# One tuned kernel, attention into a feed-forward layer: a planner that reckons with the SBUF port, q loads in five slots, weight sums in other slots

## The chip, the cores and the metric

The kernel runs on one core of one Trainium2 chip. The metric is the time of one execution on the device in microseconds (us); of several runs the median counts. TensorE (PE) multiplies, VectorE (DVE) and ScalarE (ACT) work elementwise, GpSimd (POOL) reduces over partitions here, and SyncE (SP) issues all DMAs. SBUF is the memory that these engines share, PSUM the memory that TensorE writes to; tiles lie in a fixed number of slots of a tag, and a tile waits until a slot of its tag is free.

## The reference

```
q, k, v: [8, 8, 576, 64]      w_phi: [64, 128]      w_in: [512, 2048]   w_out: [2048, 512]  (float64)

phi(x):  proj = x @ w_phi;  proj -= max|proj| over the 128 features
         return concat(exp(proj), exp(-proj))                     # 256 features
q_p, k_p = phi(q), phi(k)
kv  = sum over s of k_p[s] (x) v[s];   z = sum over s of k_p[s]
num = q_p @ kv;   den = q_p . z + 1e-6;   attn = num / den         # [8, 8, 576, 64]

x = attn as [4608, 512]
out = gelu(x @ w_in) @ w_out                                       # [4608, 512]
```

## The kernel before, in words

**Attention** goes batch by batch. For K (`k_quad`, from line 392) a quad of four heads has five units: TensorE projects into `pk`, VectorE takes the maximum `mx` (L430) and subtracts it (L334, into `pk` itself in the first two batches and into `ek` in the later ones), ScalarE takes two exponentials (`ek`, L447) and TensorE sums `kv`. For Q (`q_pair`, from line 473) a half of a pair of heads is loaded into `qt` and projected into `pq`; ScalarE copies it to `pc`, GpSimd takes the maximum over partitions (`mb`, L513), VectorE subtracts (`pc`), ScalarE takes two exponentials (`ef`, L519) and TensorE forms `pn`. From the third batch on VectorE first splits q into two parts (`qh`), GpSimd also sums over partitions (`db<-un`, L548), and `pk` and `pq` both use the one PSUM slot `pp`. `quotients` (L568, L569) sends the denominators through DRAM and takes the reciprocal `dc`.

**Feed-forward.** 32 weight tiles arrive as float64 and are turned into two float32r parts by `split_weight` (two steps on ScalarE, five on VectorE: `wt`, `w_i`, `w_o`). A block of 256 tokens loads the attention output (`xr`) and the quotients (`rb`), multiplies and splits them on VectorE (`xr`, `xh`, `xl`), and then does eight steps: 24 matmuls `ph`, two gelu on ScalarE (L635, L636), the difference `gl` on VectorE, and 12 matmuls `po`. Twelve blocks (0 to 11) go this way. The last three wide blocks of 512 tokens save matmuls with sums of weights: `combos` (line 660) builds them on VectorE (`sw`, `sh`), writes them to DRAM (`s_d`), and the wide blocks read them back into a ring (`s<-s_d`) and form `pa` and `pb`.

**What sets the order.** Every operation is first put into a list with an estimated cost and a rank. `Plan.order` plays this list through once at build time: for each engine it takes, among the operations that could start first, the one of lowest rank, and notes a start. `emit` then writes the program of every engine in the order of these starts, and nothing reorders it on the chip. In this play `start_of` (line 136) says when an operation could start, and `taken` lists the spans of the GpSimd operations. A VectorE operation marked `psum` works from PSUM; one that isn't and meets such a span is charged `BLOCKED` = 0.9 us, once for each span. The numbers at the end of the file set ranks, paces and earliest starts: `T15` and `LEAD` how far attention runs ahead of the blocks, `WPACE` the pace in which weights are released, `WR` and `WSPAN` their ranks, `TF` the earliest start of block 0, `EARLY` a shift in rank of the q side of the first batch.

Of the kernel before, what the change touches and what calls it, by code (L numbers as in the profile page):

```python
# [10 lines left out]
F32 = mybir.dt.float32  # L11
F32R = mybir.dt.float32r
# [15 lines left out]
P = 128  # L28
HS = S // 2
# [30 lines left out]
class Plan:  # L60
# [30 lines left out]
    def op(self, eng, cost, fn, r=(), w=(), also=(), rank=0.0, table=None, late=0.0, kb=0, duty=1.0, kind="f", psum=False):  # L91
        o = Op()
        o.eng, o.cost, o.fn, o.rank, o.table, o.late, o.n = eng, cost, fn, rank, table, late, len(self.ops)
        o.users, o.ready, o.nbytes, o.duty, o.kind, o.psum = [], self.since, kb, duty, kind, psum
        deps = set()
        for b in r:
            deps.update(b.writers)
        for b in w:
            deps.update(x for x in b.writers if eng != "sp" or x.eng != "sp")
            deps.update(b.readers)  # L100
        for b in r:
            b.readers.append(o)
        for b in w:
            b.writers.append(o)
        o.bufs = list(dict.fromkeys([*r, *w, *also]))
        for b in o.bufs:
            b.left += 1
        deps.update(self.gate)
        o.deps = deps
        o.wait = len(deps)  # L110
        for d in deps:
            d.users.append(o)
        if eng == "pe" and self.stream in ("k", "q"):
            o.rank += PULL
        self.ops.append(o)
        return o

    def order(self, bias):
# [17 lines left out]
        def start_of(o):  # L136
            t = max(clock[o.eng], o.ready)
            if o.table == "exp" and table[0] == "gelu" and gelus[0] % (2 * STICK):
                t = max(t, left_at[0] + PATIENCE)
            seen = {}  # L140
            for b in o.bufs:
                if not b.held and b.tag is not None:
                    f, i = slot_free_at[b.tag], seen.get(b.tag, 0)
                    if len(b.line) <= i or b.line[i] is not b:
                        return None
                    when = f[(turn[b.tag] + i) % len(f)]
                    if when is None:
                        return None
                    t = max(t, when)
                    seen[b.tag] = i + 1  # L150
            return t


# [2 lines left out]
        taken = []  # L156
# [16 lines left out]
        while len(done) < n:  # L173
            best = None
            for e, lst in cand.items():
# [3 lines left out]
                for o in lst:  # L179
                    t = start_of(o)  # L180
# [26 lines left out]
            _, t, o = best  # L207
            cand[o.eng].remove(o)
            cost = o.cost
# [3 lines left out]
            if o.eng == "pe":  # L213
                if self.SHAPE[last[0]] != self.SHAPE[o.kind]:
                    cost += self.BEHIND[last[0]] + self.BEFORE[o.kind]
                last[0] = o.kind
            if o.eng == "dve" and not o.psum:
                for span in taken[-4:]:
                    if t < span[1] - 0.3 and t + cost > span[0] + 0.3 and not span[2]:
                        span[2] = True  # L220
                        cost += BLOCKED
            if o.eng == "pool":
                taken.append([t, t + cost, False])
            o.start, o.end = t, run(t, cost, o.duty) if o.eng == "pe" else t + cost
            if o.nbytes:
                dge[0] = max(dge[0], t) + 0.55
# [6 lines left out]
            for b in o.bufs:  # L233
                if b.tag is not None and not b.held:
                    f = slot_free_at[b.tag]
# [53 lines left out]
def fused_kernel(ctx: ExitStack, tc: tile.TileContext, qT, kT, va, w_st, w_in, w_out, out):  # L289
    nc = tc.nc  # L290
# [11 lines left out]
    sb = {t: plan.pool(spool, t, n) for t, n in SLOTS.items()}  # L302
    PS = dict(pp=1, kv=1, pn=1, ph=2, po=1)
    ps = {t: plan.pool(ppool, t, n, False) for t, n in PS.items()}
    op = plan.op
# [167 lines left out]
    def q_pair(b, p, kvs, rank, halves=(0, 1)):  # L473
# [4 lines left out]
        for half in halves:  # L478
            nm = f"{b}_{p}_{half}"
            ss = slice(half * HS, half * HS + HS)  # L480
            qt = sb["qt"]([P, HS] if b < EB else [P, 2, HS], F32, f"qt_{nm}")
            if b < EB:
                op("sp", 0.06, lambda qt=qt, ss=ss: nc.sync.dma_start(out=qt(), in_=qT[b, p, :, ss]), w=[qt], kb=147, **k(1))
            else:
                for i in range(2):
                    op("sp", 0.06, lambda qt=qt, ss=ss, i=i: nc.sync.dma_start(
                        out=qt()[64 * i : 64 * i + 64], in_=qT[b, p, :, ss].rearrange("(j d) t -> d j t", j=2)), w=[qt], kb=147, **k(1))
# [4 lines left out]
            pc = sb["pc"]([P, 2, HS], F32, f"pc_{nm}")  # L492
            mb = sb["mb"]([P, 2, HS], F32, f"mb_{nm}")
# [24 lines left out]
            for s in range(2):  # L518
                op("act", act(2 * HS), lambda ef=ef, pc=pc, s=s: nc.scalar.activation(ef()[:, s], pc(), AF.Exp, scale=1.0 - 2.0 * s),  # L519
                   r=[pc], w=[ef], table="exp", **k())  # L520
# [139 lines left out]
    def combos(rank):  # L660
        plan.stream = "c"
        lo, hi = slice(0, 256), slice(256, 512)
        for q in range(4):
            for i in range(2):
                k = dict(rank=rank((2 * q + i) / 8))
                ws = [sb["ob"]([P, 512], F32, f"sw_{q}_{i}_{x}") for x in range(2)]
                hs = [sb[tag]([P, 512], F32R, f"sh_{q}_{i}_{tag}") for tag in ("db", "qt")]
                for x in range(2):
                    c = wi[i + 2 * x, q]
                    tt("dve", dve(512), ws[x], lambda c=c: c()[:, 0].bitcast(F32), lambda c=c: c()[:, 1].bitcast(F32), ALU.add, [c], [ws[x]], also=[*ws, *hs], **k)  # L670
                a, b = ws
                for to, x, y, o in (((b, hi), (b, hi), (a, hi), ALU.add), ((a, hi), (a, lo), (a, hi), ALU.subtract),
                                    ((a, lo), (b, hi), (a, lo), ALU.subtract), ((b, lo), (b, lo), (a, lo), ALU.subtract)):
                    tt("dve", dve(256), lambda to=to: to[0]()[:, to[1]], lambda x=x: x[0]()[:, x[1]], lambda y=y: y[0]()[:, y[1]], o,
                       list({x[0], y[0]}), [to[0]], **k)
                for x in range(2):
                    h, w = hs[x], ws[x]
                    copy("dve", dve(512, fast=True), h, w, [w], [h], **k)
                    tt("dve", dve(512), lambda w=w: w().bitcast(F32R), w, lambda h=h: h().bitcast(F32), ALU.subtract, [w, h], [w], **k)
                    for z, part in enumerate((h, w)):  # L680
                        for y in range(2):
                            op("sp", 0.06, lambda q=q, i=i, x=x, y=y, z=z, part=part: nc.sync.dma_start(
                                out=s_d[q]()[2 * x + y, :, :, i, z, :].rearrange("e p n -> p e n"),
                                in_=part()[:, 256 * y : 256 * y + 256].bitcast(F32).rearrange("p (e n) -> p e n", e=2)), r=[part], w=[s_d[q]], kb=131, **k)
# [3 lines left out]
    def wide_block(j, rank):  # L688
# [55 lines left out]
        for u in range(NU):  # L744
# [3 lines left out]
            sm = {}  # L748
            for s in (2, 3, 1, 4):
                m = sm[s] = sb[RING[s - 1]]([P, 2, 2, P], F32R, f"s{s}_{j}_{u}")  # L750
                op("sp", 0.06, lambda m=m, q=q, e=e, s=s: nc.sync.dma_start(out=m().bitcast(F32), in_=s_d[q]()[SUMS.index(s), e]), r=[s_d[q]], w=[m], kb=262, rank=rk - 20)
            A = ps["ph"]([P, 2, TB], F32, f"pa_{j}_{u}")
            Bk = ps[("kv", "pn")[u % 2]]([P, 2, TB], F32, f"pb_{j}_{u}")
            own = lambda c, f, q=q: (lambda i, w: wi[c + i, q]()[:, w, f % 4 * P : f % 4 * P + P], [wi[c, q], wi[c + 1, q]])
# [105 lines left out]
CR = 100.0  # L860
CSPAN = 100.0
GATE = 60
T15 = 901.4
BIAS = 40
STICK = 2
PATIENCE = 2.5
URGE = -1000.0
EARLY = 37.5
WPACE = 3.996
WSPAN = 24.5  # L870
WARM = 4
EARLY_PK = ("pp", "po")
EARLY_E = ("ek", "xh", "ek", "xl")
BLOCKED = 0.9
HOLD2 = 0.0
EB = 2
KB = 0
EPACE = 20.0
TF = 90.0
ND = 2  # L880
LUMP = 2.5
LINGER = 3.0
PAIR_K = 0.43
PAIR_Q = 0.7
PAIR_N = 1.18
PAIR_V = 0.125
PULL = -2000.0
LEAD = 167.4
HOLD = 44.6
WR = -13.5  # L890
ATR = -21.1
T0 = 57.4
VERBOSE = False


# [36 lines left out]
```

## Time and profile before

| | us |
|---|---|
| median of 3 runs | 1150.15 (1148.31 to 1151.35) |
| the profiled execution | 1147.43 |
| its span, first to last instruction | 1145.7 |
| TensorE busy | 1097.1 |
| VectorE busy | 696.2 |
| ScalarE busy | 662.2 |
| GpSimd busy | 321.5 |

TensorE is busy for 96% of the span. The mean over the span hides stages: up to 112 us there is only attention of the first batches and weight splitting, from there to some 780 us feed-forward blocks and attention are mixed, and then the feed-forward part is alone. A row of a timeline gives start, length, engine, line, operation, tiles and count, and in brackets how long the engine stood idle in front of it and what it waited for. The profile counts most fp32 matmuls twice (two passes of one instruction); the order counts them once.

### The profile page before, as it was taken

The page shows a single profiled execution, that of the slowest core. Times are in us where ns is not written, and L with a number is a line of the kernel's source. Part 1 is how long each engine was busy: PE and PEld are TensorE (multiplying, and loading weights), DVE is VectorE, ACT ScalarE, POOL GpSimd, SP SyncE. Part 2 cuts the span into 40 slices and gives each one's busy share as a digit, 9 for nine tenths or more (in the row PEclk, how much of TensorE's full clock was granted, in tenths as well). Part 3 has the DMA queues.
Part 4 walks back from the last instruction along what each step waited for, and adds up shares of the span by engine and source line. Part 5 has one row for each costly group of instructions (what it writes and reads, how often), then busy time and mean ns, then how long its engine had stood idle before and what let it go on. Part 6 is the DMA issues. An engine that isn't in the chain of part 4 may idle for free.

```text
span 1145.7 us, 22254 instructions
## 1 busy us (share of the span) xinstructions
PE 1097.1 (96%) x8952; PEld 920.4 (80%) x8952; DVE 696.2 (61%) x1153; ACT 662.2 (58%) x1045; POOL 321.5 (28%) x116
## 2 busy tenths in 40 slices
PE   7878987999999999999999999999999999999997
PEld 4545766888887888888888888889889888898986
DVE  6897889665856867656466566554655534534331
ACT  5776857767777787776878778762112222222322
POOL 3323023343644546352445445450000000000000
PEclk9998987999999999999999999999999999999999
DMA  7676631324141332413132231205543624623420
GB/s 248 222 230 215 198 104 33 95 64 129 48 124 43 93 83 86 106 62 102 55 93 80 79 88 49 69 18 125 152 129 115 190 84 115 196 94 114 136 83 37
DMA packets 112439, 125.59 MB, mean 110 GB/s; under 512 B 27648, under 2 KB 87200, under 8 KB 112336
## 3 DMA queue, kind: packets, MB, share of 16 engines
q1 hardware_dynamic: 112336, 124.17, 36.6%
q8 instruction: 70, 1.15, 0.4%
q14 instruction: 33, 0.27, 0.1%
HBM read 96.57 MB, written 27.56 MB: 108 GB/s over the span
## 4 chain that ended last, share of the span: by engine, by line
PE 72%; DVE 9%; DMA 6%; issue 4%; SPq 3%; ACT 3%; POOL 2%; DVEq 0%; ACTq 0%; POOLq 0%
PE po L308 18%; PE ph L308 18%; PE kv L308 6%; PE pb L308 5%; PE po_pp L308 5%; PE pn L308 5%; PE po_po L308 5%; PE pa L308 4%; PE pq L308 3%; PE pk L308 3%; POOL mb L513 1%; SPq L708 1%; DMA qt<-in_qT_dram 1%; DMA rp<-r_d 1%; DVE gl L334 1%
## 5 line engine op out<-in xcount | busy, mean ns | idle before, releaser
L308 PE MATMUL ph<-xh,w_i 128*128 128x256 f32 x1536 | 299.9, 284 | 1.6 <-DVE gl L334 1.2
L308 PEld LDWEIGHTS ph<-xh,w_i 128*128 128x128 f32 x1536 | 248.2, 190 | 9.6 <-issue 2.2
L308 PE MATMUL po<-w_o,gh 128*128 128x512 f32 x768 | 246.4, 402 | 1.9 <-ACT ob L328 1.9
L513 POOL PARTITION_ALL_REDUCE mb<-pc x64 | 147.8, 2311 | 285.6 <-ACT pc L328 247.1
L548 POOL PARTITION_ALL_REDUCE db<-un x48 | 175.3, 3652 | 161.6 <-DVE un L545 123.4
L308 PE MATMUL ph<-xl,w_i 128*128 128x256 f32 x768 | 218.7, 285 | 0.0
L308 PEld LDWEIGHTS po<-w_o,gh 128*128 128x128 f32 x768 | 137.7, 190 | 31.4 <-issue 2.2
L308 PE MATMUL po<-w_o,gl 128*128 128x512 f32 x384 | 152.9, 398 | 0.6 <-DVE gl L334 0.6
L308 PEld LDWEIGHTS ph<-xl,w_i 128*128 128x128 f32 x768 | 146.1, 190 | 3.3
L519 ACT ACTIVATE ef<-pc 128x576 f32<-128x576 f32 x128 | 83.1, 680 | 59.1 <-DVE pc L334 58.8
L334 DVE TENSOR_TENSOR gl<-ph,gh 128x512 fp32r<-128x512 f32 x96 | 65.8, 686 | 84.5 <-ACT ph L636 81.2
L308 PEld LDWEIGHTS kv<-vt,ek 128*64 128x64 f32 (+1 forms) x2560 | 85.6, 140 | 36.7 <-ACT ek L447 14.1
L635 ACT ACTIVATE gh<-ph 128x512 fp32r<-128x512 f32 x96 | 57.5, 599 | 90.5 <-PE ph L308 83.1
L308 PE MATMUL kv<-vt,ek 128*64 128x65 f32 (+1 forms) x2560 | 97.7, 228 | 9.6 <-ACT ek L447 9.3
L308 PE MATMUL pn<-ef,kvn 128*64 128x288 f32 (+1 forms) x512 | 98.1, 425 | 1.2 <-ACT xo L328 1.0
L635 ACT ACT_TABLE_LOAD x76 | 97.5, 1283 | 1.5 <-PE ph L308 0.3
L308 PEld LDWEIGHTS po<-w_o,gl 128*128 128x128 f32 x384 | 73.0, 190 | 18.5 <-DVE gl L334 1.6
L794 ACT ACTIVATE gh<-pa 128x512 fp32r<-128x512 f32 x24 | 14.4, 599 | 123.1 <-PE po_pp L308 86.1
L447 ACT ACTIVATE ek<-ek 128x512 f32<-128x512 f32 (+1 forms) x120 | 70.1, 587 | 24.8 <-DVE ek L334 23.0
L334 DVE TENSOR_TENSOR pc<-pc,mb 128x576 f32<-128x576 f32 x64 | 65.4, 1021 | 29.7 <-POOL mb L513 29.4
L430 DVE TENSOR_REDUCE mx<-pk 128x4 f32<-128x512 f32 (+1 forms) x80 | 50.5, 631 | 50.2 <-PE pk L308 50.0
L308 PEld LDWEIGHTS pn<-ef,kvn 128*64 128x64 f32 (+1 forms) x512 | 39.6, 139 | 32.5 <-issue 7.5
(90 smaller groups left out, 1699.5 us busy)
## 6 DMA issues: line engine op xcount, KB each, us to landing
s<-s_d SPq DMA_DIRECT2D x96, 256.0 KB
qt<-in_qT_dram SPq DMA_DIRECT2D x112, 144.0 KB
vt<-in_va_dram SPq DMA_DIRECT2D x16, 585.0 KB
kt<-in_kT_dram SPq DMA_DIRECT2D x16, 576.0 KB
out_dram<-ob SPq DMA_DIRECT2D x36, 256.0 KB
raw_i<-in_w_in_dram SPq DMA_DIRECT2D x16, 512.0 KB
raw_o<-in_w_out_dram SPq DMA_DIRECT2D x16, 512.0 KB
x_d<-xo SPq DMA_DIRECT2D x48, 144.0 KB
```

Source lines behind the costliest of these rows:

```text
L308: return tc.keep_in_program_order(nc.tensor.matmul(*a, **kw))
L334: op(eng, cost, lambda: e.tensor_tensor(out=dst(), in0=a(), in1=b(), op=o), r=r, w=w, **kw)
L430: op("dve", dve(256 * n, True), lambda xs=xs, mx=mx: nc.vector.tensor_reduce(out=mx()[:, 0].rearrange("p (j i) -> p j i", j=2), in_=xs(), ...
L447: op("act", act(256 * n, b < SB), lambda at=at, es=es, s=s: nc.scalar.activation(es[s](), at(), AF.Exp, scale=1.0 - 2.0 * s), r=[of], w=[e ...
L513: op("pool", 2.2, lambda mb=mb, pc=pc: nc.gpsimd.partition_all_reduce(mb(), pc(), P, bass_isa.ReduceOp.absmax), r=[pc], w=[mb], **k(1))
L519: op("act", act(2 * HS), lambda ef=ef, pc=pc, s=s: nc.scalar.activation(ef()[:, s], pc(), AF.Exp, scale=1.0 - 2.0 * s), r=[pc], w=[ef], ta ...
L548: op("pool", 3.7, lambda db=db, un=un: nc.gpsimd.partition_all_reduce(db(), un(), P, bass_isa.ReduceOp.add), r=[un], w=[db], **k())
L635: op("act", act(2 * TB, True) + 0.016, lambda gh=gh, ph=ph: nc.scalar.activation(gh(), ph(), AF.Gelu), r=[ph], w=[gh], table="gelu", rank= ...
L708: op("sp", 0.06, lambda b=b, i=i, h=h, s=s, n=n, o=o, z=z, to=rp[z]: nc.sync.dma_start(out=to()[64 * i : 64 * i + 64, :, o : o + n], in_=r ...
L794: op("act", act(2 * TB, psum) + 0.016, lambda gh=gh, at=at: nc.scalar.activation(gh(), at(), AF.Gelu), r=[at], w=[gh], table="gelu", rank= ...
```

## The change

The planner no longer charges `BLOCKED`. Instead a VectorE operation that is not marked `psum` cannot start, in the planner's play, inside the span of the GpSimd operation before it; it starts at that span's end. These spans are now 1.4 us for a maximum (`LOCK_MAX`) and 2.4 us for a sum (`LOCK_SUM`), in place of the whole cost of 2.2 or 3.7. The q loads of the first two batches take turns in the tags qt (one slot), gh (two) and gl (two), where they all used qt. The weight sums move from the slots ob, db and qt to ek, mb and pc, and a load of the ring now comes behind the writes of all four parts of the sums, where it came behind the one that it reads. Eleven numbers of the planner change, and with them the order on every engine. (`HOLD` has no effect, since the first two batches start at once.)

```diff
@@ start_of
+            if o.eng == "dve" and not o.psum and taken and taken[-1][0] <= t < taken[-1][1]:
+                t = taken[-1][1]
             return t
@@ order
-            if o.eng == "dve" and not o.psum:
-                for span in taken[-4:]:
-                    if t < span[1] - 0.3 and t + cost > span[0] + 0.3 and not span[2]:
-                        span[2] = True
-                        cost += BLOCKED
             if o.eng == "pool":
-                taken.append([t, t + cost, False])
+                taken.append((t, t + (LOCK_MAX if cost < 3.0 else LOCK_SUM)))
@@ q_pair
-            qt = sb["qt"]([P, HS] if b < EB else [P, 2, HS], F32, f"qt_{nm}")
+            qt = sb[("qt", "gh", "gl")[(2 * p + half) % 3] if b < EB else "qt"]([P, HS] if b < EB else [P, 2, HS], F32, f"qt_{nm}")
@@ combos
-                ws = [sb["ob"]([P, 512], F32, f"sw_{q}_{i}_{x}") for x in range(2)]
-                hs = [sb[tag]([P, 512], F32R, f"sh_{q}_{i}_{tag}") for tag in ("db", "qt")]
+                tags = ("ek", "ek") if i == 0 else ("mb", "pc")
+                ws = [sb[tag]([P, 512], F32, f"sw_{q}_{i}_{x}") for x, tag in enumerate(tags)]
+                hs = [sb[tag]([P, 512], F32R, f"sh_{q}_{i}_{x}") for x, tag in enumerate(tags)]
@@ wide_block
-                op("sp", 0.06, lambda m=m, q=q, e=e, s=s: nc.sync.dma_start(out=m().bitcast(F32), in_=s_d[q]()[SUMS.index(s), e]), r=[s_d[q]], w=[m], kb=262, rank=rk - 20)
+                op("sp", 0.06, lambda m=m, q=q, e=e, s=s: nc.sync.dma_start(out=m().bitcast(F32), in_=s_d[q]()[SUMS.index(s), e]), r=s_d, w=[m], kb=262, rank=rk - 20)
@@ numbers
-T15 = 901.4
+T15 = 1004.363
-LEAD = 167.4
+LEAD = 223.014
-BLOCKED = 0.9
+LOCK_MAX = 1.4
+LOCK_SUM = 2.4
...
```

Three places show how the order moves. The first is SyncE's queue at the start of the program: `kt` and `vt` are K and V of a quad, `qt` a half of a pair of q, `raw` a weight tile. Before:

```order
L321 DMA wst_68<-in_w_st_dram 128x128
L483 DMA qt_0_0_0_70<-in_qT_dram 128x288
L399 DMA kt_0_0_72<-in_kT_dram 128x1152
L401 DMA vt_0_0_74<-in_va_dram 128x1170
L399 DMA kt_0_1_76<-in_kT_dram 128x1152
L401 DMA vt_0_1_78<-in_va_dram 128x1170
L349 DMA raw_i0_0_80<-in_w_in_dram 128x512
L349 DMA raw_i1_0_89<-in_w_in_dram 128x512
L349 DMA raw_i2_0_97<-in_w_in_dram 128x512
L483 DMA qt_0_0_1_106<-in_qT_dram 128x288
```

and now, from the same place:

```order
L318 DMA wst_68<-in_w_st_dram 128x128
L396 DMA kt_0_0_70<-in_kT_dram 128x1152
L398 DMA vt_0_0_72<-in_va_dram 128x1170
L396 DMA kt_0_1_74<-in_kT_dram 128x1152
L398 DMA vt_0_1_76<-in_va_dram 128x1170
L480 DMA qt_0_0_0_78<-in_qT_dram 128x288
L480 DMA qt_0_0_1_80<-in_qT_dram 128x288
L480 DMA qt_0_1_0_82<-in_qT_dram 128x288
L480 DMA qt_0_2_0_85<-in_qT_dram 128x288
L346 DMA raw_i0_0_87<-in_w_in_dram 128x512
```

The first q load moves behind four K and V loads, and four q loads now stand together in front of the weights.

The second place is VectorE in block 0, around the last unit of the first quad of batch 2: `dc_1_0` is the reciprocal that `rb_2` carries to `xr_2`, and `ek_2_0_4` the subtraction that frees the PSUM slot `pp`. Before:

```order
L569 RECIPROCAL dc_1_0_1654<-dc_1_0_1654 128x18
L355 TENSOR_SCALAR wt_o10_1673<-wt_o10_1673 128x512
L334 TENSOR_TENSOR gl_0_3_1713<-ph_0_3_1638,gh_0_3_1683 128x512
...
L334 TENSOR_TENSOR w_o10_1749<-wt_o10_1673,w_o10_1749 128x512
L334 TENSOR_TENSOR xr_2_1554<-xr_2_1554,rb_2_1459 128x1024
L334 TENSOR_TENSOR gl_0_4_1790<-ph_0_4_1715,gh_0_4_1755 128x512
L353 TENSOR_SCALAR wt_o11_1797<-wt_o11_1797 128x512
L355 TENSOR_SCALAR wt_o11_1797<-wt_o11_1797 128x512
L430 TENSOR_REDUCE mx_2_0_4_1811<-pk_2_0_4_1792 128x4
L357 SCALAR_TENSOR_TENSOR wt_o11_1797<-raw_o11_1199,wt_o11_1797 128x512
L334 TENSOR_TENSOR ek_2_0_4_0_1823<-pk_2_0_4_1792,mx_2_0_4_1811 128x512
```

and now:

```order
L427 TENSOR_REDUCE mx_2_0_4_1599<-pk_2_0_4_1550 128x4
L356 SCALAR_TENSOR_TENSOR wt_o8_1521<-raw_o8_1413,wt_o8_1521 128x512
L350 TENSOR_SCALAR wt_o9_1597<-wt_o9_1597 128x512
L331 TENSOR_TENSOR ek_2_0_4_0_1614<-pk_2_0_4_1550,mx_2_0_4_1599 128x512
...
L566 RECIPROCAL dc_1_0_1601<-dc_1_0_1601 128x18
...
L331 TENSOR_TENSOR ek_2_1_1_0_1916<-pk_2_1_1_1860,mx_2_1_1_1892 128x512
L331 TENSOR_TENSOR w_i1_3_1908<-wt_i1_3_1830,w_i1_3_1908 128x512
L352 TENSOR_SCALAR wt_i2_3_1890<-wt_i2_3_1890 128x512
L331 TENSOR_TENSOR xr_2_1686<-xr_2_1686,rb_2_1580 128x1024
```

The subtraction now stands in front of the reciprocal, and `xr_2` comes 43 rows behind the reciprocal instead of 7.

The third place is VectorE at the first unit of the next quad, where `mx_2_1_0` is the maximum and `ek_2_1_0` the subtraction. Before (11 further rows stand between the first and the second of these):

```order
L430 TENSOR_REDUCE mx_2_1_0_1930<-pk_2_1_0_1888 128x4
...
L355 TENSOR_SCALAR wt_i2_3_1955<-wt_i2_3_1955 128x512
L355 TENSOR_SCALAR wt_i3_3_1976<-wt_i3_3_1976 128x512
L357 SCALAR_TENSOR_TENSOR wt_i2_3_1955<-raw_i2_3_1379,wt_i2_3_1955 128x512
L357 SCALAR_TENSOR_TENSOR wt_i3_3_1976<-raw_i3_3_1421,wt_i3_3_1976 128x512
L359 SCALAR_TENSOR_TENSOR wt_i2_3_1955<-raw_i2_3_1379,wt_i2_3_1955 128x512
L359 SCALAR_TENSOR_TENSOR wt_i3_3_1976<-raw_i3_3_1421,wt_i3_3_1976 128x512
L334 TENSOR_TENSOR ek_2_1_0_0_1995<-pk_2_1_0_1888,mx_2_1_0_1930 128x512
```

and now:

```order
L331 TENSOR_TENSOR w_o11_1777<-wt_o11_1717,w_o11_1777 128x512
L350 TENSOR_SCALAR wt_i0_3_1787<-wt_i0_3_1787 128x512
L542 SCALAR_TENSOR_TENSOR un_2_0_0_1750<-ef_2_0_0_1730,kvn_2_0_0_1411,un_2_0_0_1750 128x288
L352 TENSOR_SCALAR wt_i0_3_1787<-wt_i0_3_1787 128x512
L427 TENSOR_REDUCE mx_2_1_0_1812<-pk_2_1_0_1720 128x4
L331 TENSOR_TENSOR ek_2_1_0_0_1828<-pk_2_1_0_1720,mx_2_1_0_1812 128x512
```

Two weight tiles were split in step between the maximum and the subtraction; now the subtraction follows at once.

## Rows read from the trace of the kernel before

**Rows 1.** Busy time by stage: stretch, length, each engine's busy us, clock, DMA share, GB/s.

```profile
0.00:112.00 112.00, 89.25 (x967) 55.06 (x968) 90.40 (x149) 76.40 (x168) 32.16 (x19) 0.91 0.72 230
112.00:207.00 95.00, 82.68 (x643) 68.39 (x642) 85.21 (x136) 67.14 (x104) 26.64 (x9) 0.89 0.40 112
207.00:780.00 573.00, 571.75 (x5141) 480.30 (x5140) 357.67 (x547) 425.50 (x602) 262.68 (x89) 1.00 0.28 79
780.00:1146.00 366.00, 353.44 (x2207) 316.68 (x2206) 162.93 (x324) 93.16 (x172) 0.00 (x0) 0.99 0.40 120
```

**Rows 2.** TensorE's waits over the span: total us, times, longest us.

```profile
PE pq L308 <- DVE ek L334: 10.4, 3, 4.8
PE pq L308 <- DMA qt<-in_qT_dram: 10.1, 6, 3.8
```

**Rows 3.** TensorE in order of time, 102 to 113 us.

```profile
102.57 1.15 PE L308 MATMUL kv<-vt,ek 128*64 128x65 f32 x32
103.65 1.19 PE L308 MATMUL pn<-ef,kvn 128*65 128x288 f32 x4
104.77 0.72 PE L308 MATMUL pk<-wst,kt 64*128 64x128 f32 x8
109.26 1.33 PE L308 MATMUL pq<-qt,wst 64*128 64x288 f32 x4 [3.78 <-DMA qt<-in_qT_dram]
...
112.09 0.72 PE L308 MATMUL ph<-xh,w_i 128*128 128x256 f32 x1
```

**Rows 4.** VectorE in order of time, at 106 us.

```profile
106.33 1.23 DVE L334 TENSOR_TENSOR xr<-xr,rb 128x1024 f32<-128x1024 f32 x1 [2.98 <-DMA kt<-in_kT_dram]
```

**Rows 5.** TensorE in order of time, 153 to 177 us.

```profile
154.68 1.30 PE L308 MATMUL pq<-qh,wd 128*128 128x288 f32 x4 [3.72 <-DVE ek L334]
...
158.33 0.41 PE L308 MATMUL ph<-xh,w_i 128*128 128x256 f32 x1
158.54 0.41 PE L308 MATMUL ph<-xl,w_i 128*128 128x256 f32 x1
...
160.41 0.28 PE L308 MATMUL ph<-xl,w_i 128*128 128x256 f32 x1
160.52 0.28 PE L308 MATMUL ph<-xh,w_i 128*128 128x256 f32 x1
...
175.79 1.30 PE L308 MATMUL pq<-qh,wd 128*128 128x288 f32 x4 [4.78 <-DVE ek L334]
```

**Rows 6.** VectorE in order of time, 150 to 175 us.

```profile
150.11 1.22 DVE L334 TENSOR_TENSOR xr<-xr,rb 128x1024 f32<-128x1024 f32 x1 [3.85 <-DMA rb<-r_d]
...
168.16 3.82 DVE L353 TENSOR_SCALAR wt_i<-wt_i 128x512 f32<-128x512 f32 x2
...
174.97 0.68 DVE L334 TENSOR_TENSOR ek<-pk,mx 128x512 f32<-128x512 f32 x1
```

**Rows 7.** GpSimd's all-reduces and VectorE's steps beside them, held and not held.

```profile
42.17 2.14 POOL L513 PARTITION_ALL_REDUCE mb<-pc  x1 [2.74 <-ACT pc L328]
42.20 1.80 DVE L357 SCALAR_TENSOR_TENSOR wt_o<-raw_o,wt_o 128x512 uint32<-128x512 uint32 x1
44.04 0.69 DVE L359 SCALAR_TENSOR_TENSOR wt_o<-raw_o,wt_o 128x512 uint32<-128x512 uint32 x1
...
176.77 0.45 DVE L330 CAST qh<-qt 128x576 fp32r<-128x576 f32 x1
...
188.00 3.60 POOL L548 PARTITION_ALL_REDUCE db<-un  x1 [1.54 <-issue]
188.38 2.47 DVE L330 CAST qh<-qt 128x576 fp32r<-128x576 f32 x1
```

**Rows 8.** Around 846 us: TensorE, VectorE, and the stage's busy time as in rows 1.

```profile
846.06 0.94 PE L308 MATMUL po<-w_o,gh 128*128 128x512 f32 x2 [1.95 <-ACT ob L328]
847.15 0.69 DVE L334 TENSOR_TENSOR sw<-w_i 128x512 f32<-128x512 f32 x1 [5.20 <-DMA out_dram<-ob]
840.00:850.00 10.00, 8.05 (x45) 7.02 (x44) 4.38 (x9) 2.13 (x4) 0.00 (x0) 0.83 0.50 157
```

More of the change, by code (lines that the diff above doesn't have):

```diff
@@ L862 @@
 GATE = 60
-T15 = 901.4
+T15 = 1004.363
 BIAS = 40
 STICK = 2
-PATIENCE = 2.5
+PATIENCE = 5.704
 URGE = -1000.0
-EARLY = 37.5
-WPACE = 3.996
-WSPAN = 24.5
+EARLY = -6.886
+WPACE = 5.074
+WSPAN = 3.579
 WARM = 4
@@ L878 @@
 EPACE = 20.0
-TF = 90.0
+TF = 79.325
 ND = 2
-LUMP = 2.5
-LINGER = 3.0
+LUMP = 2.265
+LINGER = 1.639
 PAIR_K = 0.43
@@ L887 @@
 PULL = -2000.0
-LEAD = 167.4
[L889 to L892, printed above, removed]
+LEAD = 223.014
+HOLD = 71.9
+WR = -45.396
+ATR = -8.041
+T0 = 59.922
 VERBOSE = False
```

## The prediction

> **What bounds the kernel now.** I read the busy time by stage first, then the waits of TensorE, then the order of time around the longest of them. By stages [rows 1] TensorE is full from 207 to 780 us (571.75 of 573.00 us): whatever the change does there is hidden unless it makes TensorE wait. The time that can be won lies elsewhere: 112.00 - 89.25 = 22.75 us idle before the first feed-forward matmul, 95.00 - 82.68 = 12.32 us between there and 207 us, and about 12.3 us behind 780 us (353.44 busy of the 365.7 that the span still has), part of it the drain of the last outputs. In the first two stages VectorE is busy for 90.40 and 85.21 us, so it paces the start beside TensorE. The waits of TensorE [rows 2] name two causes: 10.4 us in 3 waits of pq for VectorE's write of ek, and 10.1 us in 6 waits for a q load.
>
> An idle stretch costs more than its length. After the wait of 3.72 us the feed-forward matmuls start 0.21 us apart (158.33, 158.54), at 160.41 and 160.52 again 0.11 apart [rows 5]: the granted clock fell to the lower of its two levels and came back some 5.7 us after the wait ended. Work that takes 5.7 us at half speed takes 2.85 us at full, so each such wait costs 2.8 us more.
>
> **The change part by part.** No instruction of TensorE, VectorE, GpSimd or DMA is added or dropped; order and slots change. I take the start, block 0, and the weight sums in turn, against the profiled execution (1147.43 us, 2.72 below the median of 1150.15).
>
> *Up to the first feed-forward matmul (112.09 us).* Ahead of it TensorE now has 48 more kv, 10 more pk, 4 more pn and 2 more pq matmuls. From [rows 3] 16 kv of the order (32 passes) take 103.65 - 102.57 = 1.08 us, 0.068 each; a pk 0.72/4 = 0.18; a pn (104.77 - 103.65)/2 = 0.56; a pq some 0.35. That is 3.3 + 1.8 + 2.2 + 0.7 = 8.0 us of attention done earlier. VectorE has ahead of the first xl one maximum over 512 and one over 256 more, four TENSOR_SCALAR and three SCALAR_TENSOR_TENSOR of weight splits, and three subtractions: with 0.69 per full step [rows 7] and 0.42 for the short ones about 6.6 us. So the first ph comes some 6 to 8 us later with 8 us more behind it: nothing gained or lost by order alone.
>
> What is gained there is the q loads. With one qt slot a load can't start before the pq in front has read it; with five slots it can. The wait at 109.26 was 3.78 us [rows 3], the six together 10.1 [rows 2]. What is late next is VectorE, 81% busy; it loses the 2.98 us in front of xr, when loads crowded the DMA queues [rows 4], and idles that follow TensorE's stalls. I take 4 us of gain. The bounds are the whole 10.1 us, and a loss: the first q load now stands behind four K and V loads, 128 x 1152 and 128 x 1170 floats, 2.4 MB in all, which at the stage's 230 GB/s [rows 1] need 10 us, while now the first pq runs at 8; that is up to 3 us on the q chain. Range -10 to +3.
>
> *Block 0 (112 to 207 us).* The first of the three waits: pq of batch 2 needs the PSUM slot pp, which VectorE frees with its subtraction ek. In front of that subtraction stood xr of block 2, seven rows behind the reciprocal whose result travels through DRAM to it, and it waited 3.85 us for that load [rows 6]. Now xr of block 2 stands 43 rows behind the reciprocal, far behind this ek. The second, 4.78 us [rows 5]: between the maximum and ek of the next pk stood 17 instructions, among them two weights split in step, the first held for most of 3.82 us [rows 6]; now ek follows its maximum directly. Both waits, 8.5 us, and their 5.6 us at half clock were made by what stood in front of one subtraction. What is late next is VectorE as a whole, which has the same weights to split: of its 95.00 - 85.21 = 9.8 us idle [rows 1] 3.85 is this load. Also the work that covers a handover changes: between pk and the first pq of batch 2 there were two pn and six po, now 24 ph, six po and two pn, about 2.7 us more (24 at 0.11); but between the pk in front of the second pq and that pq only 24 ph and six po stand, about 4 us, where there were 12 ph, 24 po and four pn, about 7.5 (a po at twice a ph, being twice as wide). I take half of 14, 7 us of gain. Bounds: -20 (12.3 idle and three falls of the clock all gone) to +5 (the shorter cover leaves 3.5 us open and no weight comes sooner).
>
> *VectorE and the port.* When GpSimd starts an all-reduce, a VectorE step with SBUF sources that starts then is held: a step of 0.69 took 1.80 us under the maximum begun at 42.17, a cast of 0.45 took 2.47 under the sum begun at 188.00 [rows 7]. So the port comes free about 1.2 us after the start of the maximum (42.20 + 1.80 - 0.69 - 42.17) and 2.4 after that of the sum; the changed planner reckons 1.4 and 2.4. The hold is real, but waiting for the port and being held by it take the same time: the gain is only where a PSUM step is put into the hold. In the order I do not see more PSUM steps in front of the pc subtractions than now. The 24 all-reduces up to 207 us at most (19 + 9 less four small clears, [rows 1]) at 1.2 us or more hold some 29 us; I take nothing of it, bounds -8 (a third filled, most of it off TensorE's path) and +3 (PSUM steps drawn ahead delay weights).
>
> [...]
>
> *Weight sums.* They stood in the output's ob slots: a sum waited 5.20 us for an output to leave, and TensorE 1.95 us at 846.06 for an ob copy, with the mean clock of that stretch at 0.83 [rows 8], another 10 x 0.17 = 1.7 us. In the slots of ek, mb and pc, idle by then, this goes. New is that every s load waits for all four sums, not its own. The last sum on VectorE stands four gl steps ahead of the first wide product, four layer steps of 24 ph and 12 po, about 5.3 us each, 21 us of cover; if that were gone, the first ring load would cost its own wait, some 5 us. I take 3 us of gain, range -4 to +5.
>
> ScalarE gets twenty fewer table loads; it is busy 67.14 of 95 us in block 0 and 425.50 of 573 later [rows 1], so that is worth nothing.
>
> The sum: -4 - 7 + 0 - 3 = -14 us, 1133.4 for the profiled execution, 1136 against the median.
>
> **The rivals.** *As late as before, elsewhere.* VectorE has the same work until the last weight, and where one subtraction comes sooner a weight comes later; TensorE then waits at po or ph instead of pq. For it: VectorE at 90% in block 0. Against it: 3.85 us of its idle was one misplaced load. Then only sums and part of the q loads remain, -1 to -4 us: 1148.
>
> *Short handovers (slower).* The single pp slot passes between pk and pq, and its cover before the second pq falls from 7.5 to 4 us while VectorE has weight steps between maximum and ek there. If VectorE falls over 4 us behind there, block 0 gains nothing and two waits of some 3 us come on top, each with 2.8 us of slow clock: +11.6. With the q loads at -1 (the first one late) and the sums at -3 that is +7.6: 1158. It decides from the point where VectorE's lag at the second pq is over the 4 us of cover; the order has no slack there, the trace says nothing of the lag.
>
> *All of it works.* PSUM steps do fill the holds, the waits and clock falls of block 0 go whole, the q loads give 8: -8 - 17 - 4 = -29, less what VectorE cannot follow, about -24: 1126.
>
> **How the numbers follow.** Forecast 0.48 (1130 to 1144), everything works 0.14, as late as before 0.19, short handovers 0.19. About 0.3% (3.5 us) is what a measurement of this kernel can tell from no change: faster is below 1146.7, slower above 1153.6. Faster: 0.47 of the forecast, 0.14, and 0.06 of *as late as before*: 0.67. Same: 0.01 of the forecast, 0.12 of *as late as before* and 0.03 of *short handovers*: 0.16. Slower: 0.16 of *short handovers* and 0.01 of *as late as before*: 0.17. The range leaves out about half of *all of it works* and of *short handovers*: 1122 to 1155.
>
> **What would show it.** Right: no wait of pq for a q load over 1 us; the waits of 3.72 and 4.78 us gone and the clock in 150 to 200 us at 0.95 or more; no wait for ob near 846; the first ph at 112 to 120 us. Wrong: new waits of po or ph for w_o, w_i or gl of the same sum in block 0, or of pq and pk for ek at the second pq; a wait of the first wide products for s; a held step in VectorE is no proof by itself, only TensorE's wait behind it.

## The result, and the profile after

The changed kernel takes 1132.32 us in the median of four runs (1128.54 to 1135.84), the kernel before 1149.59 beside it: ratio 0.9848, with a 95% interval of 0.9812 to 0.9884. Forecast was 1136. The profiled execution was the slowest of the four (1135.84), so the two traces lie only 11.6 us apart. The busy time by stage, as in [rows 1]:

```profile
0.00:112.00 112.00, 90.15 (x1064) 56.97 (x1064) 95.02 (x160) 81.21 (x179) 33.33 (x19) 0.95 0.68 213
112.00:207.00 95.00, 88.06 (x706) 74.03 (x703) 79.94 (x137) 65.70 (x106) 26.02 (x10) 0.98 0.52 150
207.00:780.00 573.00, 564.59 (x5033) 474.41 (x5032) 339.29 (x531) 396.60 (x573) 263.58 (x88) 0.99 0.26 75
780.00:1146.00 366.00, 344.44 (x2157) 310.20 (x2155) 162.09 (x327) 92.36 (x170) 0.00 (x0) 0.99 0.40 121
```

The clock rose from 0.91 to 0.95 and from 0.89 to 0.98 in the first two stages, and the second has 5.4 us less idle. The third stage, full before (571.75), has lost 7.2 us. TensorE's waits, as in [rows 2]:

```profile
PE pq L305 <- DVE ek L331: 9.2, 5, 4.4
PE kv L305 <- ACT ek L444: 9.2, 9, 5.1
PE pk L305 <- DVE ek L331: 5.6, 2, 3.2
PE pn L305 <- ACT xo L325: 4.8, 8, 1.1
PE pq L305 <- DMA qt<-in_qT_dram: 1.9, 1, 1.9
```

And these, of the kernel before, stand beside the two of [rows 2]:

```profile
PE kv L308 <- ACT ek L447: 9.3, 7, 2.3
PE pk L308 <- DVE ek L334: 1.1, 2, 0.6
PE pn L308 <- ACT xo L328: 1.0, 3, 0.4
```

The waits for q loads have gone from 10.1 to 1.9 us. Those of pq for VectorE's ek were 10.4 us, all between 112 and 207 us; of the 9.2 now, 5.9 lie there (4.6 in a second trace of the same order) and 3.4 behind 207 us. pk now waits 5.6 us for ek, and pn 4.8 for xo. What kv waits for ek is no different from before.

**A balance that closes.** TensorE's work is the same in all kernels, so I count what it loses, in windows of 3 us: *idle* is 3 less its busy time, *slow* its busy time times (1 - granted clock). The span less both is 1081 to 1087 us for every kernel below, so between different orders the count can be off by some 6 us. The columns give idle and slow up to 207 us, then their sum from 207 to 780 and from 780 to 1116 us, then the trace's span; ratios are those to the kernel before measured beside each (no_q_slots runs so much later that its columns cover other work).

| kernel | median | ratio (95%) | idle | slow | middle | end | span |
|---|---|---|---|---|---|---|---|
| before | 1149.59 | | 35.0 | 16.8 | 1.2 | 8.2 | 1145.7 |
| changed | 1132.32 | 0.9848 (0.9812 to 0.9884) | 28.7 | 5.6 | 11.7 | 5.3 | 1134.1 |
| changed_again | 1132.42 | 0.9873 (0.9838 to 0.9907) | 26.6 | 4.4 | 12.4 | 2.8 | 1129.5 |
| splice_ABA | 1130.20 | 0.9824 (0.9798 to 0.9849) | 25.5 | 4.9 | 4.2 | 4.0 | 1121.4 |
| splice_BAA | 1158.90 | 1.0098 (1.0072 to 1.0125) | 33.8 | 18.6 | 17.7 | 2.7 | 1154.9 |
| splice_BBA | 1146.46 | 0.9985 (0.9969 to 1.0001) | 35.3 | 20.6 | 3.9 | 3.4 | 1145.5 |
| two_moves | 1147.28 | 0.9990 (0.9971 to 1.0009) | 32.3 | 21.6 | 1.2 | 4.2 | 1143.1 |
| fewer_weight_steps | 1147.14 | 0.9982 (0.9963 to 1.0000) | 35.2 | 17.2 | 1.4 | 8.6 | 1146.1 |
| middle_moves | 1125.41 | 0.9783 (0.9761 to 0.9805) | 27.2 | 7.6 | 6.8 | 3.3 | 1127.7 |
| port_plan_alone | 1137.36 | 0.9898 (0.9870 to 0.9925) | 30.5 | 14.3 | 1.5 | 7.0 | 1137.3 |
| no_port_plan | 1124.72 | 0.9783 (0.9755 to 0.9811) | 25.0 | 9.1 | 1.8 | 5.6 | 1122.9 |
| numbers_alone | 1143.13 | 0.9946 (0.9924 to 0.9967) | 28.2 | 9.2 | 3.8 | 11.9 | 1140.5 |
| numbers_and_sums | 1136.69 | 0.9878 (0.9857 to 0.9899) | 31.5 | 7.8 | 5.6 | 4.5 | 1133.4 |
| no_q_slots | 1202.58 | 1.0455 (1.0424 to 1.0486) | 72.6 | 25.0 | 17.4 | 2.4 | 1199.8 |

Between the first two lines: -17.5 up to 207 us, of which -11.2 is clock and only -6.3 idle, +10.5 in the middle, -2.9 at the end.

### The profile page after: what moved, and what is told of

Read it like the earlier page. It is cut to its first block, busy times and chain, and to the rows that moved or that the text cites. A ratio compares the mean times of both kernels' runs of the same rounds, so it can differ in the third digit from the quotient of the medians.

```text
span 1134.1 us, 22240 instructions
## 1 busy us (share of the span) xinstructions
PE 1087.2 (96%) x8952; PEld 915.6 (81%) x8952; DVE 676.3 (60%) x1153; ACT 635.9 (56%) x1025; POOL 322.9 (28%) x116
## 5 line engine op out<-in xcount | busy, mean ns | idle before, releaser
L305 PEld LDWEIGHTS ph<-xh,w_i 128*128 128x128 f32 x1536 | 245.7, 188 | 9.9 <-issue 3.1
L305 PEld LDWEIGHTS po<-w_o,gl 128*128 128x128 f32 x384 | 72.8, 190 | 17.2 <-DVE gl L331 0.3
L792 ACT ACTIVATE gh<-pa 128x512 fp32r<-128x512 f32 x24 | 14.4, 598 | 120.7 <-PE po_pp L305 86.9
L331 DVE TENSOR_TENSOR pc<-pc,mb 128x576 f32<-128x576 f32 x64 | 53.5, 838 | 27.4 <-POOL mb L510 27.2
```

Source lines behind the costliest of these rows:

```text
L305: return tc.keep_in_program_order(nc.tensor.matmul(*a, **kw))
L331: op(eng, cost, lambda: e.tensor_tensor(out=dst(), in0=a(), in1=b(), op=o), r=r, w=w, **kw)
L792: op("act", act(2 * TB, psum) + 0.016, lambda gh=gh, at=at: nc.scalar.activation(gh(), at(), AF.Gelu), r=[at], w=[gh], table="gelu", rank= ...
```

## The experiments

An edit of a planned kernel changes the order everywhere. So eight of the twelve kernels of the experiments are not planned anew: the order is written out as a list, and only what is named is moved. The other four were planned anew and say less on single causes. A block's end is taken at its first copy of the output on ScalarE.

**Which part gains, which loses.** The orders of the two kernels were joined at the first feed-forward matmuls of blocks 2 and 8. The q slots go with the first part, the slots of the sums with the end.

```
splice_ABA   ORDER = changed[:block 2] + before[block 2:block 8] + changed[block 8:]
splice_BAA   ORDER = before[:block 2]  + changed[block 2:block 8] + changed[block 8:]
splice_BBA   ORDER = before[:block 2]  + before[block 2:block 8]  + changed[block 8:]
```

splice_ABA. 

> Written-out order: the changed kernel's up to the first feed-forward matmul of block 2 (first part), the order of before up to that of block 8 (middle), the changed kernel's again from there (end); slots of the changed kernel. Theory A (the changed order of the middle itself gives back some 8.5 us by new waits for ek and qh at 260, 342 and 467 us, while before's middle loses nothing): 1132 - 8.5 = 1124 (1121 to 1127), with TensorE's lag at block 8 no more than 1 us above that at block 2. Theory B (the middle gives back whatever was won early, because the attention of batches 2 to 7 cannot be supplied sooner by VectorE and the loads, in any order): 1131 to 1136, again with waits for ek or qh in the middle.

splice_BAA. 

> Order and q slots of before up to the first feed-forward matmul of block 2, the changed kernel's order and its slots for the weight sums from there. Theory A (each part keeps its own gain or loss: first part 0 instead of -17, changed middle +8.5, changed end -4): 1150 + 8.5 - 4 = 1154. Theory B (the middle gives back only what was won early; here nothing was): 1150 - 4 = 1146.

splice_BBA. 

> Order of before up to the first feed-forward matmul of block 8, the changed kernel's order from there, with its slots for the weight sums: the end of the change by itself. Theory (the trace's lag and the prediction's term: the wait for an ob slot near 846 us goes, with its slow clock): -3 to -4, 1146 to 1147. Rival (the last stage is bound by TensorE's products and the drain, and the sums were covered): 1149 to 1150.

With the middle of before, the middle lost 4.2 us where the changed order lost 11.7 (12.4 in a second trace); with the changed middle behind the old start it lost 17.7, and the kernel became slower than before by 0.7 to 1.25%, more than theory A's 1154. So the loss goes with the changed order of the middle and is not the early gain paid back: theory A, by the time of splice_BAA and by the traces. The time of splice_ABA doesn't show it: its median, 1130.20, missed its 1121 to 1127; its trace was the fastest of its runs (1123.18), and by ratios it is not told apart from changed_again. The end alone gave 2.0 us, and its interval just takes in no change.

**The changed kernel again.** The same instructions in the same order, as a list.

> The changed kernel once more, its order written out as a list instead of planned (the same instructions in the same order), beside the others of this call. If the middle's own waits cost the 7 to 10 us that its first trace shows between the end of block 0 and the end of block 3, every trace has them: block 0 ends about 20 us and block 3 about 10 us earlier than in before, and the median stands near 1132. If they were an accident of that one execution (the slowest of its four runs), block 3 ends 15 us or more earlier than in before, and the median is near 1128.

The end of block 3 comes 11.9 us before that of the kernel before, block 0's 23.1: the loss of the middle is in both traces, and the median is the same.

**Block 0, one step at a time.** The prediction blamed two places where something stood in front of a subtraction.

```diff
@@ VectorE, order of before
-xr_2 <- xr_2, rb_2
 ... (mx_2_0_4)
 ek_2_0_4 <- pk_2_0_4, mx_2_0_4
+xr_2 <- xr_2, rb_2
@@
 mx_2_1_0 <- pk_2_1_0
+ek_2_1_0 <- pk_2_1_0, mx_2_1_0
 ... (17 instructions)
-ek_2_1_0 <- pk_2_1_0, mx_2_1_0
```

> The kernel before with its order kept, but for two VectorE steps: the multiply of xr for block 2 stands behind the subtraction ek of the fifth K unit of batch 2 instead of in front of it, and the subtraction ek of the first K unit of the second K half stands directly behind its maximum instead of 17 instructions later (one rb load of the next block moves with the first). Theory (the prediction's account of block 0: these two steps in front of a subtraction made both long waits of pq and their falls of the clock): the waits of 3.72 and 4.78 us go, first matmul of block 2 some 8 to 13 us earlier, and 1137 to 1143 in all. Rival (VectorE as a whole sets the pace of block 0, so the waits move to po, ph or kv): block 2 no more than 3 us earlier, 1147 to 1150.

The waits for ek went, but for 0.63 us; the time did not. Block 0 ended 1.3 us later than in before, and TensorE's idle time between 112 and 207 us fell by 1.2 us only. (Most of the 4.8 us that the table has more of slow clock lie up to 112 us, where the two orders are the same: 12.2 for 8.6.) TensorE's waits in two_moves, 151 to 180 us, where [rows 5] has one of 3.72 and one of 4.78:

```profile
152.81 0.77 PE L310 MATMUL pq<-qh,wd 128*128 128x288 f32 x4 [0.63 <-DVE ek L336]
...
165.69 0.96 PE L310 MATMUL po<-w_o,gh 128*128 128x512 f32 x2 [1.20 <-ACT gh L637]
167.89 0.79 PE L310 MATMUL po<-w_o,gl 128*128 128x512 f32 x1 [1.24 <-DVE gl L336]
175.77 0.38 PE L310 MATMUL ph<-xh,w_i 128*128 128x256 f32 x1 [1.81 <-ACT w_i L330]
...
178.90 1.33 PE L310 MATMUL pq<-qh,wd 128*128 128x288 f32 x4 [1.16 <-ACT pc L330]
```

All but the first are now for something else: gelu, gl, a weight, the copy pc. VectorE at the place where ek_2_1_0 used to stand:

```profile
169.61 2.26 DVE L355 TENSOR_SCALAR wt_i<-wt_i 128x512 f32<-128x512 f32 x1 [0.41 <-ACT wt_i L354]
171.79 1.47 DVE L357 TENSOR_SCALAR wt_i<-wt_i 128x512 uint32<-128x512 uint32 x2
173.18 1.28 DVE L359 SCALAR_TENSOR_TENSOR wt_i<-raw_i,wt_i 128x512 uint32<-128x512 uint32 x2
174.39 1.28 DVE L361 SCALAR_TENSOR_TENSOR wt_i<-raw_i,wt_i 128x512 uint32<-128x512 uint32 x2
175.75 1.35 DVE L336 TENSOR_TENSOR w_i<-wt_i,w_i 128x512 fp32r<-128x512 f32 x2
```

The same two weights are split there, and they end no sooner for the subtraction having gone ahead; the ph at 175.77 needs their parts. That looked like an engine that is simply full, so the next kernel took work from it.

```diff
@@ split_weight, order of before
-        op("dve", ..., lambda: v.tensor_scalar(... scalar1=F64_MIN, scalar2=F64_MAX, op0=ALU.max, op1=ALU.min), ...)
+        op("dve", ..., lambda: [], ...)
```

> The kernel before in its own order, with one of the two TENSOR_SCALAR steps of each weight left out (the clamp of the magnitudes): 32 steps of 0.418 us, 13.4 us of VectorE's work, nearly all of it ahead of 207 us. Theory V (VectorE's whole work sets the pace up to the end of block 0, whatever single step TensorE is seen waiting for): block 0 ends 9 to 13 us earlier, 1136 to 1141. Rival (single steps in front of a subtraction set it): block 0 ends less than 3 us earlier, 1146 to 1150.

That reading fell as well: block 0 ended 0.3 us earlier, with VectorE busy for 160.3 us up to 207 instead of 175.6. It had as many weights ready at 170 us as before (26), and the order still made it wait. VectorE in fewer_weight_steps (its wait for xr_2 is there as well, and the pq at 155.02 waited 3.35 us):

```profile
161.86 0.18 DVE L569 TENSOR_SCALAR dc<-dc 128x18 f32<-128x18 f32 x1 [3.13 <-DMA dc<-d_d]
...
169.74 3.82 DVE L356 TENSOR_SCALAR wt_i<-wt_i 128x512 uint32<-128x512 uint32 x2
173.47 1.27 DVE L358 SCALAR_TENSOR_TENSOR wt_i<-raw_i,wt_i 128x512 uint32<-128x512 uint32 x2
174.67 1.28 DVE L360 SCALAR_TENSOR_TENSOR wt_i<-raw_i,wt_i 128x512 uint32<-128x512 uint32 x2
175.88 0.68 DVE L336 TENSOR_TENSOR ek<-pk,mx 128x512 f32<-128x512 f32 x1
```

VectorE stood idle for 3.13 us for a transfer, then met a held pair of weights 1.6 us later than in before (169.74 for 168.16), and the pq at 176.70 waited 5.32 us. So in block 0 several chains end within a few microseconds of each other, and neither a place in the order nor an amount of work moves the end by itself. Both together were not tried. What goes with the gain is the number of weights ready at 170 us, counted in the timelines: 26 in before, two_moves and fewer_weight_steps, 28 to 30 in changed, changed_again, numbers_alone and no_port_plan. That this is the cause is not shown; port_plan_alone had 25 there and won 7.0 us in the first part.

**The middle, three places.** In the changed kernel VectorE is busy for 339.29 of 573 us in the middle, so there a single order mistake should count. VectorE and TensorE of the changed kernel near 258 us:

```profile
253.24 0.69 DVE L331 TENSOR_TENSOR ek<-pk,mx 128x512 f32<-128x512 f32 x1
257.74 1.23 DVE L331 TENSOR_TENSOR xr<-xr,rb 128x1024 f32<-128x1024 f32 x1 [3.81 <-DMA rb<-r_d]
258.89 0.17 DVE L565 TENSOR_SCALAR dc<-dc 128x18 f32<-128x18 f32 x1
258.96 0.69 DVE L427 TENSOR_REDUCE mx<-pk 128x4 f32<-128x512 f32 x1
259.56 0.26 DVE L566 RECIPROCAL dc<-dc 128x18 f32<-128x18 f32 x1
259.74 0.64 DVE L331 TENSOR_TENSOR ek<-pk,mx 128x512 f32<-128x512 f32 x1
```

```profile
258.07 0.28 PE L305 MATMUL ph<-xh,w_i 128*128 128x256 f32 x1
260.52 0.77 PE L305 MATMUL pq<-qh,wd 128*128 128x288 f32 x4 [2.17 <-DVE ek L331]
```

It is the picture of [rows 6] at another place: the multiply of xr waits for a load, and the maximum and the subtraction stand behind it.

```diff
@@ VectorE, order of changed (first of three places)
-xr_4 <- xr_4, rb_4
-dc_2_1 (sum)
 mx_3_0_4 <- pk_3_0_4
-dc_2_1 (reciprocal)
 ek_3_0_4 <- pk_3_0_4, mx_3_0_4
+xr_4 <- xr_4, rb_4
+dc_2_1 (sum), dc_2_1 (reciprocal)
```

> The changed kernel with its written-out order, but for VectorE in three places of the middle: xr of block 4 and the two dc steps behind it stand behind the ek of the fifth K unit of batch 3 (at 255 us), the maximum and ek of the first K unit of batch 4 stand in front of three un steps and a pc subtraction (at 335 us), and xr of block 7 with four dc steps stands behind ek and qh of batch 5 (at 456 us). TensorE, ScalarE and GpSimd keep their order; two DMAs move by a row or two. Theory (in the middle VectorE has time to spare, and three steps that wait for a transfer or another engine in front of a subtraction make TensorE's waits of 2.7, 2.1 and 1.8 us and the slow clock behind them, 3.2 us): 1132 - 8 to 10 = 1122 to 1124, TensorE's idle and slow time between 207 and 780 us from 12 to 3 us. Rival (as in block 0, the waits only move): 1130 to 1133.

VectorE in middle_moves at the same place:

```profile
255.39 0.69 DVE L429 TENSOR_REDUCE mx<-pk 128x4 f32<-128x512 f32 x1 [1.44 <-PE pk L307]
256.11 0.69 DVE L333 TENSOR_TENSOR ek<-pk,mx 128x512 f32<-128x512 f32 x1
257.76 1.22 DVE L333 TENSOR_TENSOR xr<-xr,rb 128x1024 f32<-128x1024 f32 x1 [0.95 <-DMA dc<-d_d]
```

The subtraction comes 3.6 us earlier and xr not later (257.76 for 257.74). The median is 7.0 us lower than that of changed_again, the intervals of the ratios clear of each other, though 1125.41 misses the expected 1122 to 1124 and the middle keeps 6.8 us of loss in the trace, which is the slowest of its runs. TensorE's waits at the first and the third place (2.17 us for ek, 1.8 for qh) are gone; at the second the wait of pk (2.38) is gone, but the next handover, the pq at 342.31, now waits 1.81 us for its ek. The same kind of move that was worth nothing in block 0 is worth some half of the loss here, by the traces and by the medians.

**The port, the numbers, the slots.** These were planned anew, but for no_q_slots.

```diff
@@ port_plan_alone: before with
-                        cost += BLOCKED        (and its test)
+            if o.eng == "dve" and not o.psum and taken and taken[-1][0] <= t < taken[-1][1]: t = taken[-1][1]
@@ no_port_plan: changed, with the same lines the other way round
@@ numbers_alone: before with
-T15 = 901.4 ... T0 = 57.4
+T15 = 1004.363 ... T0 = 59.922
@@ numbers_and_sums: numbers_alone with the sums' new slots
@@ no_q_slots: changed, order kept as far as the slot allows, with
-            qt = sb[("qt", "gh", "gl")[(2 * p + half) % 3] if b < EB else "qt"](...)
+            qt = sb["qt"](...)
```

port_plan_alone. 

> The kernel before, planned with the new rule of the port and nothing else: old numbers, old slots. Theory P: held time of VectorE in the first 207 us from 20 to 12 to 15 us, block 0 ends 5 to 10 us earlier, 1139 to 1144. Rival (the port is worth nothing by itself): 1146 to 1152.

no_port_plan. 

> The changed kernel, planned with the old rule of the port (each VectorE step with SBUF sources beside an all-reduce costs 0.9 us more, once per all-reduce) instead of waiting until the port is free; numbers and slots of the changed kernel. The planner's order differs from the start. Theory P (VectorE's pace bounds the first part, and the steps put into the holds are the gain): VectorE's held time in the first 207 us back from 11.5 to about 20 us, block 0 ends 7 to 10 us later than in the changed kernel, 1139 to 1144. Rival (the prediction: the port is worth nothing; what counts is the order of the attention and of the weights): 1130 to 1135.

Alone on the old numbers the port rule gave 13.5 us against the kernel before measured beside it (1150.83; 8.4 us between the traces); on top of the new numbers and slots it cost 7.7 (1124.72 without, 1132.42 with, measured side by side, intervals apart). What VectorE's steps take beyond the usual length of their shape, counted over 0.25 us up to 207 us, is 23.4 us in before, 14.4 with the rule alone, 14.3 in the changed kernel and 19.5 without the rule (the expectations' 20 and 11.5 come from a narrower count). So the rule does what it says, and the kernel with more held time is still the faster one of the two with the new numbers and slots. The stages of no_port_plan:

```profile
0.00:112.00 112.00, 92.33 (x1017) 55.89 (x1018) 94.76 (x156) 81.42 (x177) 35.98 (x20) 0.92 0.71 222
112.00:207.00 95.00, 89.69 (x699) 75.75 (x698) 83.99 (x143) 67.98 (x107) 23.90 (x8) 0.98 0.49 136
207.00:780.00 573.00, 571.12 (x5164) 481.75 (x5163) 334.40 (x530) 401.32 (x580) 265.81 (x88) 1.00 0.27 76
```

Its first part loses 34.1 us, as the changed kernel's does (34.3 and 31.0), and its middle is full.

numbers_alone. 

> The kernel before planned with the sixteen changed numbers and nothing else: old rule of the port, one slot for q loads, sums in the old slots. Theory N (what gains is the order that the numbers make: more of the attention ahead of block 0): block 0 ends 15 us or more earlier than in before, 1126 to 1134. Rival (the numbers need the slots; with one slot the early q loads wait): 1140 to 1150.

numbers_and_sums. 

> The kernel without the port plan (1124.7) with its q loads back in the one slot, planned anew: numbers and the slots of the sums, old rule of the port. Theory Q (the q slots are worth some 4 us where the planner may arrange the rest): 1127 to 1131, waits of pq for a q load 6 us or more. Rival (nothing, since VectorE sets the pace): 1123 to 1126.

no_q_slots. 

> The changed kernel with its written-out order, but with all q loads back in the one slot qt; only what that slot forbids stands later (loads, and up to 98 of 1153 VectorE steps, all before block 1 ends). Theory (the prediction's term: the slots are worth the waits of TensorE for q loads, 4 us): waits of pq for the load back at 6 to 10 us, 1136 (1134 to 1140). Rival (VectorE's splitting of weights sets the pace of the first part, and those waits lie beside it): 1130 to 1133, in spite of the waits.

Thirteen numbers change, HOLD among them (the counts named earlier are off). By themselves they take the first part's loss from 51.8 to 37.4, but the end loses 3.7 us more, and the whole is 5.8 lower. The sums' slots then give 6.4 us: the end's loss falls from 11.9 to 4.5, the other columns rise by 3.7. The q slots, planned anew, give 12.0 (1136.69 to 1124.72, not measured side by side), of which 5.2 in the first part. Taken out of an order that was made for them, the q slots cost 70 us (up to 98 VectorE steps had to stand later for it); neither theory had that. TensorE's largest waits of no_q_slots up to 200 us and VectorE's largest, then the same wait of VectorE in changed_again:

```profile
PE pn L307 <- ACT ef L518: 31.1, 6, 5.6
PE pq L307 <- DMA qt<-in_qT_dram: 15.6, 6, 8.2
DVE pc L333 <- POOL mb L512: 35.6, 7, 9.1
```

```profile
DVE pc L333 <- POOL mb L512: 2.8, 2, 2.0
```

With one slot the next half of q can't even be loaded before its slot is read. TensorE's waits for the loads themselves are the smaller part; VectorE waits for the all-reduce, and TensorE for the exponentials behind it. My reading is that copy, all-reduce, subtraction and exponentials of one half then run bare, and that everything that the order put behind them waits on every engine; no run parts this from the VectorE steps that stand later.

no_port_plan and middle_moves beat both kernels (0.9783 each); they are not told apart.

## Why the prediction was right, and where not

*Up to the first feed-forward matmul, -4.* Loss up to 112 us went from 31.3 to 26.1, and 23.0 in the second trace: a gain of the forecast's size or more, for another reason. The q loads' waits left as told (one of 1.88 us stayed at the first pq, at 10.60, as the bound had it, over the 1 us named as a sign), yet idle fell by 0.9 to 2.7 us only. What came late next was not VectorE alone: up to 112 us pn waits 4.2 us for ScalarE's xo where it waited 0.7, and pk 3.2 for VectorE's ek where it waited for none. The first ph came at 115.95 us (112.73 in the second trace), 3.9 and 0.6 us later and not 6 to 8. All the traces with one of the two orders up to there say the same: with that of before (before, splice_BAA, splice_BBA, two_moves) idle is 19.8 to 22.7 us and slow 8.6 to 12.7, with that of the changed kernel (changed, changed_again, splice_ABA, middle_moves) idle is 19.7 to 21.8 and slow 3.0 to 6.0. So the gain up to 112 us is clock, not idle; why the new order keeps the clock up is not shown. And "nothing gained or lost by order alone" fell: numbers_alone won 14.4 us up to 207 us with one q slot.

*Block 0, -7.* From 20.5 to 8.2 us of loss: -12.3, inside the bounds (the loss is 8.0 in the second trace). The step that failed is its reason: "both waits, 8.5 us, and their 5.6 us at half clock were made by what stood in front of one subtraction". Moving just these two took the waits away and nothing else. Nor did the changed kernel lose both: the second is gone, but its pq at 155.92 waits 4.41 us for ek. VectorE took the maximum in front of that ek only 6.5 us after pk was done (147.06 to 153.55), with ten steps ahead of it, one of them a dc that waited 1.97 us for its transfer. The clock from 150 to 200 us was 0.97 all the same. The rival *as late as before, elsewhere* describes two_moves; by what part of its order the changed kernel escaped it stays open.

*The port, 0.* Wrong in both surroundings, by -13.5 and by +7.7, both outside the bounds. That a hold and a wait for it take the same time was my estimate; no run tests it by itself. The runs showed that the rule also makes another order, whose worth depends on the numbers and slots around it: with the new ones the middle loses 1.8 us without the rule and 11.7 and 12.4 with it, so the loss of the middle came with the order that the rule made. How much of the 13.5 is order and how much shorter holds is not shown: with the rule alone held time fell by 9.0 us and the first part's loss by 7.0.

*The middle, "hidden unless it makes TensorE wait".* It did, by 10.5 us, and the order in hand showed the places: xr, un and dc in front of ek. I looked for this only in block 0, where moving such steps alone gave nothing.

*Sums, -3.* No ob wait near 846 us, no wait for s of the first wide product; 2.9 and 5.4 us less loss in the two traces, 2.0 in splice_BBA (by itself not clear of no change), 6.4 on the new numbers. Right.

The sum of -14 met -17.3 by medians because block 0 won more than forecast, and the middle, for which nothing was taken, gave much of it back. That these two errors nearly cancel is luck.

## What to carry to other kernels

A wait that ends last is worth its length only where the next chain is far behind: in block 0 two long waits could be removed for nothing, while three shorter ones, where VectorE was 59% busy, gave 7 us. Test such a reason with one step moved in a frozen order; planning anew changes everything at once, and its parts don't add (-13.5 alone, +7.7 on top). Look for in-order steps that wait for a transfer in front of a step that TensorE needs in the full stages too, since what is hidden there is hidden only as long as the order stays.

## What the runs showed of the hardware

A fall of the clock has no fixed price. These are the windows around one wait of pq in before (3.72 us, pq at 154.68) and one in the changed kernel (4.41 us, pq at 155.92); the number ahead of the last two is the granted clock (in before, by half microseconds, 1.00 up to 153.5 us, 0.50 from 154.0 to 160.0 and 1.00 again from 160.5 on):

```profile
153.00:156.00 3.00, 1.32 (x5) 1.36 (x6) 2.93 (x7) 1.26 (x2) 0.00 (x0) 0.58 0.68 173
156.00:159.00 3.00, 3.00 (x10) 2.41 (x10) 2.82 (x3) 1.78 (x3) 2.20 (x1) 0.50 0.35 129
159.00:162.00 3.00, 3.00 (x44) 2.80 (x45) 1.96 (x5) 0.07 (x1) 0.60 (x1) 0.78 0.03 3
```

```profile
153.00:156.00 3.00, 0.08 (x1) 0.12 (x1) 3.00 (x7) 1.79 (x3) 0.00 (x0) 0.97 0.75 219
156.00:159.00 3.00, 3.00 (x36) 2.68 (x36) 3.00 (x6) 2.99 (x5) 0.00 (x0) 0.50 0.19 76
159.00:162.00 3.00, 3.00 (x22) 2.66 (x19) 0.98 (x3) 0.62 (x1) 2.81 (x1) 0.96 0.57 151
```

Behind the longer wait the slow clock cost less: busy time times what the clock lacks is 1.6 us in its three windows, against 2.7 in before. And with the same order up to block 2, the slow clock took 8.6 us up to 112 us in before's trace, but 12.3 and 12.7 in splice_BAA and splice_BBA: 4 us between executions of the same instructions.

The traces show holds of VectorE and no port; the port is my word for their cause. In before all 53 steps between SBUF tiles that start within 1 us behind the start of an all-reduce take 0.4 us or more beyond the usual length of their shape, and the 24 that work on a PSUM tile (12 gl, 8 mx, 3 ek, 1 pk) take their usual length to 0.02 us. In the changed kernel 44 of 47 take that much more, and none of the 33 on a PSUM tile.

The planner's 1.4 and 2.4 us fit the trace of before. Over all VectorE steps up to 760 us that took 0.4 us or more beyond the usual length of their shape while an all-reduce ran, the time beyond it was over 1.4 us (median of 46) after the start of a maximum, whose span is 2.3 us, and 2.5 us (27) after that of a sum, whose span is 3.7. GpSimd's spans are rough, and some holds lasted longer: that of the pair at 168.16 of [rows 6] to some 3.5 us after its sum began (167.67).

VectorE and ScalarE ran in the order of the program: their 1153 and 893 steps stand in before's trace as they stand in it. The 1280 kv instructions left 2560 matmuls and 2560 weight loads there, the 2304 ph one of each.
